# A second score buffer for the first units, the first loads in parts, and routing pieces turned by transposing DMAs

## The chip, the cores and the metric

One NeuronCore of a Trainium2 chip runs the whole program. The core has a matrix engine (TensorE, PE in the profile, with its weight loads as PEld), a vector engine (VectorE, DVE), an activation engine (ScalarE, ACT), a general engine (GpSimd, POOL) and a synchronisation engine (SyncE, SP) that mostly issues DMAs. SBUF is the on-chip memory, PSUM the banks into which PE accumulates. The metric is the device time of one execution in microseconds (us); lower is better.

## What is computed

Three stages follow each other; the second and third take the rows that the one before made.

```python
# 1: attention over 4 batches x 8 heads, 576 rows of 64; scores within tau of the row's maximum are kept
scores = scale * q @ k.T
thresh = max(scores, -1) - tau
scores = where(scores >= thresh, scores, -1e9)
attn = exp(scores - max(scores)) / (sum + 1e-9)
x = (attn @ v)                     # laid out as 2304 x 512
# 2: the mixture
h = x @ w_in                       # 512 -> 2048
x = (h - tanh(h)) @ w_out          # 2048 -> 512
# 3: the experts, one per row
logits = x @ w_gate;  e_idx = argmax(logits, 1)     # 8 experts
gate_w = softmax(logits)[e_idx];  eom = sigmoid(x @ w_output_gate)
for e in range(8):                 # rows with e_idx == e only
    out[mask] = gate_w * eom[:, e] * (relu(x[mask] @ w1[e]) @ w2[e])     # 512 -> 1024 -> 512
```

## The kernel before

The order of all work is made when the program is built, by a list planner written in Python (class `Sched`). Each operation is added with `sc.add(engine, planned duration, due time, function, reads, writes)`; a DMA with `dma(...)`, which adds the issue on its queue. Buffers are rings: `buf(pool, tag, n, shape)` gives the next of n buffers, and its first writer waits for the users of the one n places back. The planner walks through all operations greedily, in several rounds, and writes an order for each engine; each engine then runs its own in order. So a change of one operation, of a buffer count or of a due time moves rows on every engine.

**Attention.** There are 32 units, each of one batch, one half of the rows and one pair of heads, with 4 or 5 tiles of 128 rows. For one tile PE makes the scores into a PSUM buffer `sp` of two banks (L939 in the first 8 units, L928 later), DVE takes the row's minimum of the negated scores and copies them to `em` (L948), ACT makes the exponential `e` (L951), ACT or POOL the threshold `tb` (L955, L959), DVE masks and multiplies (L961), PE transposes the result in four blocks (L998, L1015), ACT copies it out as `eth` (L422), and PE multiplies with v (L1030). There is one `sp` buffer: the scores of a tile wait until DVE has read those of the tile before. `raw_k`, `raw_v` and `raw_q` load k, v and q; the first q goes over the queue of ACT (L864), and tau over that of POOL (L393).

**Mixture.** The rows are cut in 9 chunks of 256. A step (`step`) takes a slice of the hidden size: PE makes `ph` (L604), ACT and DVE the function, PE adds it to two PSUM tiles `x2_0` and `x2_1` (L638). Some steps of chunks 0 to 6 run between attention units, with their PSUM pools `ps_x` (2 banks) and `ps_h` (1 bank) open from the start, beside the pools `ps_s`, `ps_t` and `ps_v` of the attention. Partial sums go to DRAM (`x2p`). After the attention the chunks are finished in the order of

```python
ORDER = ((7, 6), (0,), (1,), (2,), (3,), (4,), (5,), (8,))
```

**Routing.** `route` runs for each finished chunk, over its two tiles of 128 rows. DVE adds up or copies the tile into `xr` in SBUF (L690, L693), and SP stores it to DRAM as `x2f` (L694). PE turns `xr` in four blocks of 128x128 back into the same PSUM tile (L698), ACT takes the first bf16 piece `xs0` from there (L709), DVE the remainder `xd` (L711), DVE or ACT the second piece, DVE or POOL the third (L716). PE multiplies each piece with the gate weights in four matmuls (L723, tile `rt`), and from the logits come ranks (L769) and at last the lists of rows of each expert (L831). The last chunk routed, 8, is kept whole: it is turned too and goes straight on in f32.

**Experts.** `early_rows` reads the list that stands after chunk 5, gathers expert 0's rows from `x2f` by two indirect DMAs on POOL (L1162), and PE transposes them (L1169) for the first layer of expert 0 (L1193). The other experts follow to the end of the program.

Of the kernel before, what the change touches and what calls it, by code (L numbers as in the profile page):

```python
# [12 lines left out]
BF16 = mybir.dt.bfloat16  # L13
# [8 lines left out]
P = 128  # L22
# [27 lines left out]
HALVE = 400  # L50
FULL = 8
NHH = 12
NRAW = 2
# [268 lines left out]
def tile_main(ctx, tc, qa, qb, q2, kT, k3, vv, tau, w_in, w_out, gates, w1, w2, out, dbg=None):  # L322
# [69 lines left out]
    ext_m = sc.mem()  # L392
    nc.gpsimd.dma_start(tau_t, tau.to_broadcast([P, 1]))  # L393
    nc.scalar.activation(usum[:, 0:1], bsq, AF.Exp)
# [65 lines left out]
    a_ps = ExitStack()  # L460
    pools["ps_x"] = pool("ps_x", PS, stack=a_ps)
    pools["ps_h"] = pool("ps_h", PS, stack=a_ps)
    a_stack = ExitStack()
# [4 lines left out]
    for n_ in ("ps_s", "ps_t", "ps_v"):  # L468
        pools[n_] = pool(n_, PS, stack=at_stack)

# [204 lines left out]
    def route(c, due, x2, part, listed=True):  # L675
# [9 lines left out]
        for t in range(2):  # L685
            T = 2 * c + t
            xr = buf("rt", "xr", 3, [P, DM])
            if part:
                dma(due - 20000, lambda xr=xr, T=T: nc.sync.dma_start(xr.t, x2p[T]), [x2p_m[T]], [xr], 262144)
                sc.add("DVE", dve(512, True) + 5, due, lambda xr=xr, t=t: nc.vector.tensor_tensor(  # L690
                    out=xr.t, in0=x2[t].t, in1=xr.t, op=ALU.add), [x2[t]], [xr])
            else:
                sc.add("DVE", dve(512, True), due, lambda xr=xr, t=t: nc.vector.tensor_copy(xr.t, x2[t].t), [x2[t]], [xr])  # L693
            dma(due, lambda xr=xr, T=T: nc.sync.dma_start(x2f[T * P:(T + 1) * P, :], xr.t), [xr], [(x2f_m, T)], 262144)  # L694

            def turns(xr=xr, t=t):
                for k in range(4):
                    nc.tensor.transpose(x2[t].t[:, k * P:(k + 1) * P], xr.t[:, k * P:(k + 1) * P], ident)  # L698

            sc.add("PE", 434, due, turns, [xr], [x2[t]])  # L700
            xd = buf("rt", "xd", 2, [P, DM])
            if whole:
                xts.append(xd)
                sc.add("ACT", act(512, True), due, lambda xd=xd, t=t: nc.scalar.activation(
                    xd.t, x2[t].t, AF.Copy), [x2[t]], [xd])
                continue
            xs = [buf("rt", f"xs{k}", 2, [P, DM], BF16) for k in range(3)]
            xts.append(xs)
            sc.add("ACT", act(512, True), due, lambda xs=xs, t=t: nc.scalar.activation(  # L709
                xs[0].t, x2[t].t, AF.Copy), [x2[t]], [xs[0]])  # L710
            sc.add("DVE", dve(512, True) + 5, due, lambda xs=xs, xd=xd, t=t: nc.vector.tensor_tensor(  # L711
                out=xd.t, in0=x2[t].t, in1=xs[0].t, op=ALU.subtract), [x2[t], xs[0]], [xd])
            round_to("r_2", 512, due, lambda xs=xs: xs[1].t, lambda xd=xd: xd.t, [xd], [xs[1]])
            eng = pick("r_3")
            e_ = nc.vector if eng == "DVE" else nc.gpsimd
            sc.add(eng, dve(512) + 5 if eng == "DVE" else pool_tt(512), due, lambda xs=xs, xd=xd, e_=e_: e_.tensor_tensor(  # L716
                out=xs[2].t, in0=xd.t, in1=xs[1].t, op=ALU.subtract), [xd, xs[1]], [xs[2]], port=True)
        lg = buf("ps_r", "rt", 1, [P, 2, 48])
        g_, gr = gt_
        for t in range(2):  # L720
            def logits(k, t=t):
                for cc in range(4):
                    nc.tensor.matmul(  # L723
                        lg.t[:, t, 0:48 - 16 * k], xts[t][k].t[:, cc * P:(cc + 1) * P], g_.t[:, cc, 0:48 - 16 * k],
                        start=(k == 0 and cc == 0), stop=(k == 2 and cc == 3))
# [122 lines left out]
    def raw_k(b, hp, due):  # L848

        k_ = kst[b, hp] = buf("kv", "kst", 4, [P, 2, S])  # L850
        dma(due - 6000, lambda: nc.sync.dma_start(
            k_.t.rearrange("p a b -> p (a b)")[:, 0:3 * KB], k3[b, hp]), (), [k_], 3 * P * KB * 4)

# [4 lines left out]
    def raw_q(ui, due):  # L858
# [4 lines left out]
        eng = nc.sync if ui else nc.scalar  # L863
        dma(due - 6000, lambda: eng.dma_start(  # L864
            qh.t[:, 0:n], q2[b, hp, :, o:o + n]), (), [qh], 512 * n, "SP" if ui else "ACT")
        return qh, None
# [29 lines left out]
    def attention(ui, k0, qs):  # L896
# [12 lines left out]
        for qt in range(2 + half):  # L909
# [4 lines left out]
            for h in range(1 if merged else 2):  # L914
                d = T0 + k * TAU
                k += 1
                sp = buf("ps_s", "sp", 1, [P, 2, 512])
                mx = buf("sm", "mx", 8, [P, 1])
# [25 lines left out]
                if full:  # L944
                    sc.add("PE", 880, d - TAU // 2, scores_full, [qh, kb], [sp])
                else:
# [143 lines left out]
    for ui, (b, half, hp) in enumerate(units):  # L1090
# [20 lines left out]
        if ui < 4 and FULL < 8:  # L1111
            prep_k(b, hp, (starts[ui + 4] - 4) * TAU)
        sc.kind = "moe"
        for c in range(NCH):
            if ready[c] == ui:
# [668 lines left out]
```

## Time and profile before

| | us |
|---|---|
| runs, median (lowest to highest) | 986.95 (985.33 to 987.18) |
| the profiled execution | 984.61 |
| its span | 982.8 |
| PE busy | 950.9 |
| DVE busy | 708.2 |
| ACT busy | 560.0 |
| POOL busy | 400.1 |

The span is from the first to the last instruction in the profiler's record of one execution. Busy times of several engines overlap. The attention fills the time to some 480 us, with parts of the mixture between its units, the rest of the mixture and the routing run from there to some 735 us, and the experts to the end.

### The profile page before, as it was taken

To read this page: it belongs to the slowest core of one execution; us is meant where nothing else is said; L and a number is where in the kernel's file an instruction comes from. 1 tells how busy PE (TensorE), PEld (TensorE's weight loads), DVE (VectorE), ACT (ScalarE), POOL (GpSimd) and SP (SyncE) were. 2 spreads that over 40 slices of the span, in tenths; PEclk is the share of its full clock that TensorE was granted. 3 is DMA by queue.
4 is the path that set the end of the run, shared out by engine and by line. 5 is a ranking of instruction groups with operands and counts; after the bars stand their busy time and mean duration, and the time that the engine had idled before them with its cause. 6 is when DMAs were issued, how large, how long until landed. Compare 5 with 4: busy or idle time off the path is not lost.

```text
span 982.8 us, 18693 instructions
## 1 busy us (share of the span) xinstructions
PE 950.9 (97%) x6655; PEld 817.4 (83%) x6655; DVE 708.2 (72%) x1744; ACT 560.0 (57%) x1186; POOL 400.1 (41%) x603
## 2 busy tenths in 40 slices
PE   6889899999999999999999999999999999999997
PEld 3456678888888888888889888888898889999996
DVE  5889999989779775665278986698556786666630
ACT  5678878888787866766355434444333443444431
POOL 2457988889778865644300110011102320122101
PEclk9899999999999999999999999999999999999999
DMA  7365553654654762532582842231714766565501
GB/s 235 132 212 165 186 192 138 199 182 155 200 198 137 235 206 73 173 136 103 221 324 83 291 149 87 97 119 54 260 41 152 262 229 217 172 191 183 185 1 42
DMA packets 45015, 162.56 MB, mean 165 GB/s; under 512 B 6142, under 2 KB 6142, under 8 KB 39024
## 3 DMA queue, kind: packets, MB, share of 16 engines
q1 hardware_dynamic: 41472, 151.11, 46.0%
q0 software_dynamic: 3296, 9.90, 2.9%
q8 instruction: 54, 0.88, 0.4%
q10 hardware_dynamic: 144, 0.26, 0.1%
q14 instruction: 49, 0.40, 0.1%
HBM read 126.12 MB, written 35.59 MB: 165 GB/s over the span
## 4 chain that ended last, share of the span: by engine, by line
PE 81%; DVE 9%; issue 3%; ACT 2%; POOL 2%; DMA 1%; POOLq 0%; SPq 0%; DVEq 0%; ACTq 0%
PE ph L604 18%; PE x L638 18%; PE ph L1556 10%; PE py L1443 7%; PE pv L1030 7%; PE sp L928 6%; PE pt L998 5%; PE py L1589 3%; DVE em L961 3%; DVE em L948 2%; PE ph L1193 1%; DVE ct L552 1%; PE sp L939 1%; DVE ct L555 1%; PE pt L1488 1%
## 5 line engine op out<-in xcount | busy, mean ns | idle before, releaser
L604 PE MATMUL ph<-xh,wi 128*128 128x256 f32 x1152 | 181.8, 287 | 0.0
L638 PE MATMUL x<-wo,gh 128*128 128x512 f32 x576 | 169.0, 405 | 0.6 <-POOL gh L424 0.6
L961 DVE SCALAR_TENSOR_TENSOR em<-em,tb,e 128x576 f32<-128x576 f32 x144 | 140.5, 978 | 31.6 <-ACT e L951 18.0
L604 PEld LDWEIGHTS ph<-xh,wi 128*128 128x128 f32 x1152 | 156.8, 189 | 5.3 <-issue 0.9
L951 ACT ACTIVATE e<-em,mx 128x576 f32<-128x576 f32 x144 | 111.0, 772 | 46.3 <-DVE em L948 40.9
L948 DVE TENSOR_SCALAR_CACHE_REDUCE em<-sp 128x576 f32<-128x576 f32 x144 | 108.3, 752 | 36.8 <-PE sp L928 23.5
L424 POOL TENSOR_SCALAR gh<-u 128x512 fp32r<-128x512 f32 x52 | 40.2, 773 | 191.2 <-DVE u L627 128.0
L638 PEld LDWEIGHTS x<-wo,gh 128*128 128x128 f32 x576 | 98.9, 189 | 17.6 <-issue 1.8
L422 ACT ACTIVATE eth<-pt 128x512 f32<-128x512 f32 (+1 forms) x160 | 85.5, 549 | 24.8 <-PE pt L998 24.6
L998 PE MATMUL pt<-ident,em 128*128 128x128 f32 x576 | 88.6, 279 | 6.4 <-DVE em L961 4.2
L604 PE MATMUL ph<-xl,wi 128*128 128x256 f32 x576 | 94.5, 286 | 0.0
L638 PE MATMUL x<-wo,gl 128*128 128x512 f32 x288 | 92.8, 405 | 0.0
L617 ACT ACTIVATE u<-ph 128x512 f32<-128x512 f32 x72 | 42.8, 594 | 87.4 <-PE ph L604 81.2
L998 PEld LDWEIGHTS pt<-ident,em 128*128 128x128 f32 x576 | 68.8, 143 | 20.2 <-DVE em L961 10.1
L625 DVE SCALAR_TENSOR_TENSOR w<-w,u 128x512 f32<-128x512 f32 x72 | 51.4, 713 | 41.4 <-ACT w L621 41.1
L604 PEld LDWEIGHTS ph<-xl,wi 128*128 128x128 f32 x576 | 78.8, 189 | 1.1 <-issue 0.8
L442 DVE TENSOR_TENSOR w<-wraw,w 128x512 fp32r<-128x512 f32 x98 | 66.1, 692 | 11.8 <-ACT w L422 10.0
L928 PE MATMUL sp<-kst,qh 128*128 128x288 f32 (+2 forms) x252 | 72.9, 308 | 1.6 <-DVE em L948 1.4
L1030 PE MATMUL pv<-eth,vt 128*64 128x256 f32 (+1 forms) x512 | 70.9, 417 | 1.0 <-ACT elh L422 1.0
L1477 POOL DMA_INDIRECT rows<-x2f,gid x20 | 21.9, 1096 | 116.4 <-PE pt L1488 109.6
L928 PE MATMUL sp<-kst,ql 128*128 128x288 f32 (+2 forms) x252 | 67.9, 293 | 0.0
L638 PEld LDWEIGHTS x<-wo,gl 128*128 128x128 f32 x288 | 51.0, 189 | 9.7 <-issue 0.9
(372 smaller groups left out, 2051.2 us busy)
## 6 DMA issues: line engine op xcount, KB each, us to landing
wraw<-in_w_dram SPq DMA_DIRECT2D x64, 512.0 KB, 4.3
wi<-wsv SPq DMA_DIRECT2D x17, 1024.0 KB, 6.0
wo<-wsv SPq DMA_DIRECT2D x17, 1024.0 KB, 5.4
craw<-in_w_in_dram SPq DMA_DIRECT2D x14, 512.0 KB, 4.1
craw<-in_w_out_dram SPq DMA_DIRECT2D x14, 512.0 KB, 3.8
kr<-in_kT_dram SPq DMA_DIRECT2D x24, 288.0 KB, 4.4
wsv<-wi SPq DMA_DIRECT2D x6, 1024.0 KB, 4.3
wsv<-wo SPq DMA_DIRECT2D x6, 1024.0 KB, 5.6
```

Of the source, the lines that this page charges most:

```text
L422: return sc.add("ACT", act(n, psum), due, lambda: nc.scalar.activation(dst(), src(), AF.Copy), r, w)
L442: return sc.add(eng, dve(n, psum) + 5 if eng == "DVE" else pool_tt(n), due, lambda: e.tensor_tensor(out=dst(), in0=src(), in1=hi().bitcast ...
L604: nc.tensor.matmul(ph.t[:, j, :], wi.t[:, w_, cc * CH + j * P:cc * CH + (j + 1) * P], x_.t[:, cc, :], start=(n == 0 and cc == 0), stop=(n ...
L638: nc.tensor.matmul(x2b[c, half][t].t, g_.t[:, j, t * P:(t + 1) * P], wo.t[:, w_, j * DM:(j + 1) * DM], start=(first and n == 0 and j == 0) ...
L928: nc.tensor.matmul(sp.t[:, kb_, o:o + w], q_.t[:, q0:q0 + P], kb.t[:, hh, c0:c0 + w], start=(i == 0), stop=(i == len(todo) - 1),)
L948: sc.add("DVE", 665, d, lambda ev=ev, sp=sp, mx=mx: nc.vector.tensor_scalar(out=ev().rearrange("p (a b) -> p a b", a=2), in0=sp.t[:, :, 0: ...
L951: sc.add("ACT", 667, d + 800, lambda e=e, ev=ev, mx=mx: nc.scalar.activation(e.t, ev(), AF.Exp, bias=mx.t, scale=-1.0), [(em, h), mx], [e])
L961: sc.add("DVE", 729, d + TAU, lambda ev=ev, tb=tb, e=e, rs=rs, h=h: nc.vector.scalar_tensor_tensor(out=ev(), in0=ev(), scalar=tb.t, in1=e. ...
L998: nc.tensor.matmul(pt.t[:, kt, :], em.t[:, c0:c0 + P], ident, is_transpose=True, start=(kt == 0), stop=(kt == 3))
L1030: nc.tensor.matmul(pvf()[h * D:(h + 1) * D], vb_.t[:, k, :], eth[h].t[:, kt, 0:n] if kt < 4 else elh.t[:, 0:n], start=(kt == 0), stop=(kt ...
L1443: nc.tensor.matmul(py[k].t[:, 0:cap], wx()[:, k * P:(k + 1) * P], x_.t[:, 0:cap], start=(f == 0 and n == 0), stop=(f == 7 and n == 2))
L1556: nc.tensor.matmul(ph.t[:, 0:cap], wx()[:, cc * P:(cc + 1) * P], x_.t[:, cc, 0:cap], start=(n == 0 and cc == 0), stop=(n == 2 and cc == 3))
```

## The change

It has two parts that the diff keeps apart.

The first is at the start of the program. A pool `ps_e` with a second `sp` buffer takes the banks of `ps_x` and `ps_h` for units 0 to 3 (`EARLY`), in which every other tile uses it; a barrier (`to_a`) closes it after unit 3 and opens the mixture's pools, and the steps are held behind that barrier (`sc.gate`). The first load of k is cut into three parts, the third due later, the first load of q into two, and the scores depend on the parts that they read. The load of tau goes from POOL's queue to ACT's.

The second is in `route`. For the eight chunks routed before the last, PE does not turn `xr`. The pieces are made from `xr` in SBUF, and each bf16 piece of 128x512 is turned by a DMA that transposes while it copies (`dma_start_transpose`, on SP) into `xt`, from which the logits read. The last chunk keeps its turns on PE. The ring of `xr` goes from 3 buffers to 2, those of the pieces from 2 to 1, and `xt` has 2 of each.

```diff
+EARLY = 4
-    nc.gpsimd.dma_start(tau_t, tau.to_broadcast([P, 1]))
+    nc.scalar.dma_start(tau_t, tau.to_broadcast([P, 1]))
...
-    pools["ps_x"] = pool("ps_x", PS, stack=a_ps)
-    pools["ps_h"] = pool("ps_h", PS, stack=a_ps)
+    e_ps = ExitStack()
+    pools["ps_e"] = pool("ps_e", PS, stack=e_ps)
...
+    def to_a():
+        e_ps.close()
+        pools["ps_x"] = pool("ps_x", PS, stack=a_ps)
+        pools["ps_h"] = pool("ps_h", PS, stack=a_ps)
...
-            xr = buf("rt", "xr", 3, [P, DM])
+            xr = buf("rt", "xr", 2, [P, DM])
...
-            sc.add("PE", 434, due, turns, [xr], [x2[t]])
             xd = buf("rt", "xd", 2, [P, DM])
             if whole:
+                def turns(xr=xr, t=t):
...
+                sc.add("PE", 434, due, turns, [xr], [x2[t]])
                 xts.append(xd)
...
-            xs = [buf("rt", f"xs{k}", 2, [P, DM], BF16) for k in range(3)]
-            xts.append(xs)
-            sc.add("ACT", act(512, True), due, lambda xs=xs, t=t: nc.scalar.activation(
-                xs[0].t, x2[t].t, AF.Copy), [x2[t]], [xs[0]])
-            sc.add("DVE", dve(512, True) + 5, due, lambda xs=xs, xd=xd, t=t: nc.vector.tensor_tensor(
-                out=xd.t, in0=x2[t].t, in1=xs[0].t, op=ALU.subtract), [x2[t], xs[0]], [xd])
+            xs = [buf("rt", f"xs{k}", 1, [P, DM], BF16) for k in range(3)]
+            xt_ = [buf("rt", f"xt{k}", 2, [P, 4, P], BF16) for k in range(3)]
+            xts.append(xt_)
+            sc.add("ACT", act(512), due, lambda xs=xs, xr=xr: nc.scalar.activation(
+                xs[0].t, xr.t, AF.Copy), [xr], [xs[0]])
+            sc.add("DVE", dve(512) + 5, due, lambda xs=xs, xd=xd, xr=xr: nc.vector.tensor_tensor(
+                out=xd.t, in0=xr.t, in1=xs[0].t, op=ALU.subtract), [xr, xs[0]], [xd], port=True)
...
+            for k in range(3):
+                dma(due, lambda k=k, xs=xs, xt_=xt_: nc.sync.dma_start_transpose(xt_[k].t, xs[k].t), [xs[k]], [xt_[k]],
+                    262144, slack=600)
...
-                        lg.t[:, t, 0:48 - 16 * k], xts[t][k].t[:, cc * P:(cc + 1) * P], g_.t[:, cc, 0:48 - 16 * k],
+                        lg.t[:, t, 0:48 - 16 * k], xts[t][k].t[:, cc, :], g_.t[:, cc, 0:48 - 16 * k],
...
+        first = not (b or hp)
+        for j0, n, d in ((0, 1, 0), (1, 1, 0), (2, 1, TAU)) if first else ((0, 3, 0),):
...
+        for h in range(2 if not ui else 1):
+            cols = slice(h * 256, h * 256 + 256) if not ui else slice(0, n)
...
-                sp = buf("ps_s", "sp", 1, [P, 2, 512])
+                sp = buf("ps_e" if ui < EARLY and k % 2 == 0 else "ps_s", "sp", 1, [P, 2, 512])
...
+        if ui == EARLY - 1:
+            open_a = sc.barrier(to_a, 0, list(sc.ops))
...
+                    sc.gate = open_a
                     e_ = step(c, v[0], i == 0, i == n - 1, "ps_h", "ps_x", moe_due, span, "ga", 0)
+                    sc.gate = None
```

The planner's new orders are shown at four places. First PE at the start of the program, before and then now; a tile's scores are one row, `pt` and `pv` are transposes, the numbers tell buffers apart:

```order
L939 MATMUL sp_246<-kst_224,qh_222 128x288 x2
L939 MATMUL sp_260<-kst_224,qh_222 128x288 x2
L998 MATMUL pt_265<-ident_60,em_253 128x128 x4
L939 MATMUL sp_276<-kst_224,qh_222 128x288 x2
L998 MATMUL pt_286<-ident_60,em_253 128x128 x4
L1015 MATMUL pv_295<-ident_60,em_253 128x128
L939 MATMUL sp_300<-kst_224,qh_222 128x288 x2
```

```order
L956 MATMUL sp_234<-kst_221,qh_219 128x288 x2
L956 MATMUL sp_245<-kst_221,qh_219 128x288 x2
L956 MATMUL sp_260<-kst_221,qh_219 128x288 x2
L956 MATMUL sp_273<-kst_221,qh_219 128x288 x2
L1016 MATMUL pt_280<-ident_60,em_248 128x128 x4
L956 MATMUL sp_290<-kst_225,qh_227 128x288 x2
L1016 MATMUL pt_300<-ident_60,em_248 128x128 x4
```

Four tiles' scores stand ahead of the first transposes now, where two stood. Next ACT at its start, before and now:

```order
L864 DMA qh<-in_q_dram 128x512
L394 ACT_TABLE_LOAD
L394 ACTIVATE usum<-bsq 128x1
L951 ACTIVATE e<-em,mx 128x576 x2
L544 ACTIVATE ct<-craw 128x512
```

```order
L394 DMA tau_t<-in_tau_dram 128x1
L395 ACT_TABLE_LOAD
L395 ACTIVATE usum<-bsq 128x1
L880 DMA qh<-in_q_dram 128x256 x2
L969 ACTIVATE e<-em,mx 128x576 x3
```

The q loads stand behind the table load and an activation, where the one q load stood first. Next PE at the first routed chunk, before and now (`x_0` and `x_1` are the two x2 tiles, `rt` the logits):

```order
L638 MATMUL x_1_7042<-wo_7272,gl 128x512 x2
L698 MATMUL x_0_7024<-ident,xr 128x128 x4
L638 MATMUL x_1_6797<-wo_7272,gl 128x512 x2
L604 MATMUL ph<-xh,wi_6618 128x256 x4
L604 MATMUL ph<-xl,wi_6618 128x256 x4
L604 MATMUL ph<-xh,wi_6618 128x256 x4
L698 MATMUL x_1_7042<-ident,xr 128x128 x4
L723 LDWEIGHTS xs_7422
L723 MATMUL rt<-g_6965,xs_7422 128x48
```

```order
L644 MATMUL x_0_7532<-wo_6672,gh 128x512 x4
L644 MATMUL x_0_7532<-wo_6672,gl 128x512 x2
L644 MATMUL x_1_7544<-wo_6672,gh 128x512 x4
L644 MATMUL x_1_7544<-wo_6672,gl 128x512 x2
L610 MATMUL ph<-xh,wi_7166 128x256 x4
L733 LDWEIGHTS xt_7435
L733 MATMUL rt<-g_7037,xt_7435 128x48
```

The turns are gone, and the logits of a tile stand behind later steps' matmuls: between a tile's last x2 matmul and its first logits there are from 40 matmuls of 256 columns with 22 of 512 up to three times as many. Last SP where the routing begins, before and now (`x2f` is the store of a tile, `wraw`, `wi` and `wo` are weights):

```order
L525 DMA wo_9485<-wsv_1_205 128x2048
L525 DMA wi_9522<-wsv_0_208 128x2048
L525 DMA wo_9547<-wsv_1_207 128x2048
L525 DMA wo_9597<-wsv_1_209 128x2048
L694 DMA x2f<-xr 128x512 x2
```

```order
L726 DMA_TRANSPOSE xt_7435<-xs_7423 128x4x128
L700 DMA x2f<-xr 128x512
L726 DMA_TRANSPOSE xt_7478<-xs_7469 128x4x128
L726 DMA_TRANSPOSE xt_7493<-xs_7476 128x4x128
L1301 DMA wraw<-in_w_dram 128x1024
L531 DMA wo_7509<-wsv_1_208 128x2048
```

Three transposing DMAs for each tile stand between stores and weight loads now, 48 in all, where SP had the stores alone.

## Rows read from the trace of the kernel before

**Rows 1.** The page, section 1: busy us, share of the span, instructions.

```profile
PE 950.9 (97%) x6655; PEld 817.4 (83%) x6655; DVE 708.2 (72%) x1744; ACT 560.0 (57%) x1186; POOL 400.1 (41%) x603
```

**Rows 2.** Windows: stretch, us, busy per engine, TensorE clock, DMA share, GB/s.

```profile
0.00:60.00 60.00, 44.53 (x254) 25.36 (x255) 44.55 (x127) 36.76 (x74) 22.10 (x51) 0.94 0.57 182
60.00:120.00 60.00, 55.58 (x380) 36.68 (x378) 55.91 (x128) 50.47 (x107) 47.78 (x72) 0.97 0.60 186
120.00:180.00 60.00, 57.93 (x422) 47.74 (x420) 57.28 (x125) 49.23 (x108) 51.64 (x77) 1.00 0.48 162
180.00:240.00 60.00, 59.51 (x432) 50.19 (x432) 53.84 (x119) 49.72 (x107) 51.22 (x77) 1.00 0.63 201
600.00:660.00 60.00, 59.99 (x467) 53.08 (x467) 44.39 (x164) 24.18 (x52) 6.89 (x8) 1.00 0.30 106
```

**Rows 3.** Timeline of PE, first and last of 16 turns: start us, us, instruction.

```profile
553.96 0.60 PE L698 MATMUL x<-ident,xr 128*128 128x128 f32 x4
554.31 0.71 PE L638 MATMUL x<-wo,gl 128*128 128x512 f32 x2
...
686.20 0.60 PE L698 MATMUL x<-ident,xr 128*128 128x128 f32 x4
686.63 0.26 PE L723 MATMUL rt<-g,xs 128*128 128x48 bf16 x4
```

**Rows 4.** Groups by line and form, 480 to 730 us: busy us, mean ns, idle before.

```profile
L711 DVE TENSOR_TENSOR xd<-x,xs 128x512 f32<-128x512 f32 x16 | 10.9, 684 | 1.1 <-ACT xs L709 1.1
L716 POOL TENSOR_TENSOR xs<-xd,xs 128x512 bf16<-128x512 f32 x8 | 9.8, 1224 | 36.1 <-DVE xs L426 29.5 <-PE rt L775 6.6
L709 ACT ACTIVATE xs<-x 128x512 bf16<-128x512 f32 x16 | 9.5, 596 | 19.7 <-PE x L698 18.2 <-DVE xs L426 1.5
```

**Rows 5.** DMA issues: count, KB each, median us from issue to landing.

```profile
x2f<-xr SPq DMA_DIRECT2D x18, 256.0 KB, 2.0
x2p<-xo SPq DMA_DIRECT2D x14, 256.0 KB, 6.2
xr<-x2p SPq DMA_DIRECT2D x14, 256.0 KB, 2.7
...
qh<-in_q_dram SPq DMA_DIRECT2D x3, 256.0 KB, 4.6
...
rows<-x2f,gid POOLq DMA_INDIRECT x20, 4.0
```

**Rows 6.** Chain of waits, 510 to 530 us: start us, us, what.

```profile
519.69 2.87 PE ph L604 x24
522.56 2.79 PE x L638 x12
```

**Rows 7.** Timeline around the list and the gathers of expert 0.

```profile
696.40 0.22 PE L831 MATMUL lst<-pb,pa 128*128 128x48 bf16 x2
...
701.09 1.01 POOL L1162 DMA_INDIRECT xd<-x2f,ge  x1 [0.30 <-issue]
...
723.50 1.04 PE L1169 MATMUL x<-ident,xd 128*128 128x128 f32 x8
```

**Rows 8.** Waits of DVE, 0 to 60 us: total us, times, longest us.

```profile
DVE em L948 <- PE sp L939: 6.5, 4, 5.0
DVE em L961 <- ACT e L951: 3.3, 4, 1.0
...
DVE em L961 <- ACT tb L955: 1.0, 1, 1.0
...
DVE em L961 <- POOL tb L959: 0.7, 1, 0.7
```

**Rows 9.** Timeline of the first microseconds.

```profile
0.73 0.39 ACTq L864 DMA_DIRECT2D qh<-in_q_dram  x1
...
1.16 1.28 ACT L394 ACT_TABLE_LOAD   x1 [1.16 <-PEq L1773]
...
5.32 0.53 PEld L939 LDWEIGHTS sp<-kst,qh 64*128 64x128 f32 x4 [5.32 <-DMA qh<-in_q_dram]
```

More of the change, by code (lines that the diff above doesn't have):

```diff
@@ L468, in tile_main @@
     for n_ in ("ps_s", "ps_t", "ps_v"):
-        pools[n_] = pool(n_, PS, stack=at_stack)
+        pools[n_] = pool(n_, PS, side="right", stack=at_stack)
+    def to_a():
+        e_ps.close()
+        pools["ps_x"] = pool("ps_x", PS, stack=a_ps)
+        pools["ps_h"] = pool("ps_h", PS, stack=a_ps)
     xc = {}
@@ L694, in route @@
             dma(due, lambda xr=xr, T=T: nc.sync.dma_start(x2f[T * P:(T + 1) * P, :], xr.t), [xr], [(x2f_m, T)], 262144)
-            def turns(xr=xr, t=t):
-                for k in range(4):
-                    nc.tensor.transpose(x2[t].t[:, k * P:(k + 1) * P], xr.t[:, k * P:(k + 1) * P], ident)
-            sc.add("PE", 434, due, turns, [xr], [x2[t]])
             xd = buf("rt", "xd", 2, [P, DM])
             if whole:
+                def turns(xr=xr, t=t):
+                    for k in range(4):
+                        nc.tensor.transpose(x2[t].t[:, k * P:(k + 1) * P], xr.t[:, k * P:(k + 1) * P], ident)
+                sc.add("PE", 434, due, turns, [xr], [x2[t]])
                 xts.append(xd)
@@ L850, in raw_k @@
         k_ = kst[b, hp] = buf("kv", "kst", 4, [P, 2, S])
-        dma(due - 6000, lambda: nc.sync.dma_start(
-            k_.t.rearrange("p a b -> p (a b)")[:, 0:3 * KB], k3[b, hp]), (), [k_], 3 * P * KB * 4)
+        first = not (b or hp)
+        for j0, n, d in ((0, 1, 0), (1, 1, 0), (2, 1, TAU)) if first else ((0, 3, 0),):
+            cols = slice(j0 * KB, (j0 + n) * KB)
+            dma(due - 6000 + d, lambda cols=cols: nc.sync.dma_start(
+                k_.t.rearrange("p a b -> p (a b)")[:, cols], k3[b, hp, :, cols]), (),
+                [(k_, j) for j in range(j0, j0 + n)], n * P * KB * 4)
     def raw_v(b, hp, due):
@@ L863, in raw_q @@
         eng = nc.sync if ui else nc.scalar
-        dma(due - 6000, lambda: eng.dma_start(
-            qh.t[:, 0:n], q2[b, hp, :, o:o + n]), (), [qh], 512 * n, "SP" if ui else "ACT")
+        for h in range(2 if not ui else 1):
+            cols = slice(h * 256, h * 256 + 256) if not ui else slice(0, n)
+            dma(due - 6000, lambda cols=cols: eng.dma_start(
+                qh.t[:, cols], q2[b, hp, :, o + cols.start:o + cols.stop]), (),
+                [(qh, j) for j in ((h,) if not ui else (0, 1))], 512 * (cols.stop - cols.start), "SP" if ui else "ACT")
         return qh, None
@@ L944, in attention @@
                 if full:
-                    sc.add("PE", 880, d - TAU // 2, scores_full, [qh, kb], [sp])
+                    sc.add("PE", 880, d - TAU // 2, scores_full,
+                           [(qh, 0), (qh, 1), (kb, 0), (kb, 2)] if merged else [(qh, h), (kb, h)], [sp])
                 else:
```

## The prediction

> **What bounds the kernel now.** I read the page's busy times first, then the busy time by stretch, then who waits for whom in the stretches that the change touches. TensorE (PE) is busy for 950.9 of 982.8 us [rows 1], so some 32 us of the span are left in which it does nothing. The stretches say where [rows 2]: the first 60 us hold 44.53 us of PE work, so 15.5 us of the 32 are there; 60 to 120 lacks 4.4 and 120 to 180 another 2.1 us, and VectorE (DVE) stands at 55.91 and 57.28 of 60 in these. From 180 us on PE is nearly full (59.51), and 600 to 660 us, in the middle of the routing, shows 59.99 of 60. Two rules follow. In the routing the time falls by what is taken off PE, one for one, and an operation on another engine costs nothing until PE waits for it. At the start the time falls only if the idle time of PE shrinks, and behind the first microseconds that goes by DVE, which holds the attention back there.
>
> The profiled execution took 984.61 us for a span of 982.8 us; the median of the runs is 986.95 us. I make the sum against 984.61 and add 2.34 us at the end.
>
> **Part 1, the routing.** Of nine chunks of 256 rows eight lose their turns on PE: 2 tiles each, so 16 groups of four 128x128 transposes. The rows show the first and the last of these [rows 3]. From the start of a group to the start of the next work on PE it is 0.35 us at 553.96, 0.43 at 686.20. Over all 16 the sum is 6.4 us (the modelled ends overlap, so the distance of the starts is the price, not the 0.60 us of the row). None of it hides behind anything, because PE is full there [rows 2]. The term is **-6.4 us**.
>
> What is added: the pieces are made out of SBUF in place of PSUM, by the same operations in the same number (ACT 596 ns, DVE 684 ns, POOL 1224 ns, [rows 4]); ACT has 24 of 60 us to do there and DVE 44 [rows 2], so I cost a different source at nothing. Each tile then issues three transposing DMAs on SP, 48 in all, and the logits matmul takes their result. In the trace no such DMA appears. The nearest rows are moves of 256 KB, twice the size of a bf16 piece: the x2f store lands 2.0 us after its issue, loads of that size 2.7 to 4.6 us, a gather of 128 scattered rows 4.0, the slowest store 6.2 [rows 5]. I take 2.7 (a load into SBUF in the same stretch; ends 2.0 and 6.2). It costs time only if PE reaches the logits first. From a tile's last x2 matmul to its third piece it is xr, xs0, xd, xs1, xs2: 0.7 + 0.6 + 0.7 + 0.6 + 1.2 = 3.8 us (xr as xd, xs1 as xs0), and I put the handing over at 0.6 us more; with 2.7 us of DMA that is 7.1 us. The new order leaves between a tile's last x2 matmul and its first logits at the tightest place 40 matmuls of 256 columns and 22 of 512. The pace of PE is 2.87 us for 24 and 2.79 us for 12 [rows 6], so that is 4.8 + 5.1 = 9.9 us; elsewhere it is 10 to 31 us. So even 5.5 us of landing would be covered, and I cost the wait at nothing. The end of 6.2 us costs 0.7 us at the tight place, and 0 elsewhere.
>
> One advance is to be looked at apart: the list of expert 0's rows comes from the last of the routed chunks that count for it, and the gathers wait for it. Before, the list's matmul starts at 696.40, the second gather issues at 701.09, PE takes the gathered rows at 723.50 [rows 7]. With 4.0 us to land [rows 5] the chain is 8.7 us long, and 27 us stood there. In the new order 48 matmuls of 256 columns and 22 of 512 stand there, 5.7 + 5.1 = 10.9 us. So 2.2 us of slack are left of some 18; no cost, but this cover is thin.
>
> SP is moved past too: 48 issues stand between stores and weight loads. A transposing DMA waits on SP for its piece, and behind it stand the next weight loads (the order shows a wraw and a wo behind the first tile's three). The wait ends when the piece is there, some microseconds at most, and the loads are issued well ahead of use; cost nothing, end +2 us.
>
> Here a rule of the notes speaks against the change. The rows give 0.35 and 0.43 us for a group of four transposes on PE [rows 3]. The Trainium skill, VectorE: DVE Perf Modes, section on the three transpose paths, puts a 128x128 bf16 transpose at 390 ns on TensorE and at 1309 ns through the DMA crossbar, so the change trades a cheap path for a dear one. An estimate by that page is 4 x 1309 ns = 5.2 us for a piece: covered by the 5.5 us above if the three pieces of a tile fly together, but 48 x 5.2 = 251 us if they go one at a time (rival D would then end near 1085 us). No run here shows it yet.
>
> **Part 2, the start.** The order shows PE with the scores of four tiles ahead of the first transposes, where it had two, and DVE with the next tile's row minimum (L948) in the place of a wait. In the first 60 us DVE waits 6.5 us for scores, 5.0 of them ahead of the very first tile, which a second buffer cannot help; 1.5 us remain. For the exponential on ACT it waits 3.3 us and for the threshold 1.7 [rows 8]. A DVE that has another tile's scores lying ready can fill all of these: 1.5 + 3.3 + 1.7 = 6.5 us. But the buffer serves units 0 to 3 only, the weight conversions that used to fill such holes move to later rows, and the mixture's first steps may not start until unit 3 is done, since its banks lend the buffer. I take half of it and a little: **-3.5 us**, ends 0 and -6.5. It reaches the end because DVE is the fuller engine until past 120 us, with PE short of work [rows 2], so all behind it comes earlier.
>
> **Part 3, the first loads.** Before, ACT issues the q load at 0.73 us, ahead of its table load at 1.16 (1.28 us), and PE's first weight load waits for q until 5.32 us: 4.6 us from issue [rows 9]. Now the tau load stands first, then the table load and one activation, then two half loads of q. So the q issue slips to about 2.65 us, the second half to 3.0. With 2.7 us to land it is there at 5.7, with 2.0 at 5.0, with the 4.6 of the crowded start at 7.6. The first k parts are a third as large and are early enough. I take 5.7, **+0.4 us**, ends -0.3 and +2.3. What the earlier issue of tau saves is inside part 2's 1.7 us for thresholds and not counted twice.
>
> **The sum.** -6.4 - 3.5 + 0.4 = -9.5 us, so 984.61 - 9.5 = 975.1 in the profiled execution's terms and 977.5 us as a median.
>
> **Rivals.** (A) The forecast, -5 to -14 us: 973 to 982 us.
>
> (B) The start does not do what it says: the planner's new order, the gate on the mixture's steps and the later q load eat the gain. Then the routing's -6.4 us is left, give or take 2: 979 to 983 us. For it speaks that the gate keeps PE from filling holes in the stretch with most of them; against it that DVE, not PE, is behind there.
>
> (C) No difference: a little of everything, late logits at some tiles, a start that loses 2 to 5 us since q comes at 7.6 us and steps start later. 985 to 989 us.
>
> (D) Slower: the transposing DMAs run one after another. From the first turn at 553.96 [rows 3] to expert 0's list at 696.40 [rows 7] there are 142.4 us for 48 of them, 3.0 us each. With the slack of 2.2 us at the list and the 9.5 us gained it ends above the time before from 154/48 = 3.2 us each. At 4.0 us, the gather's time [rows 5], it is 192 - 142 = 50 us of lateness, less 12: some 1025 us. At 2.7 us nothing is seen. Against it: the DMA engines were busy for 0.30 of 600 to 660 us [rows 2], so transfers have room to run side by side. For it: nothing here shows the transposing kind.
>
> (E) Slower by a little: expert 0's rows come late. Above 2.2 us of slip each microsecond costs one on PE, so a list that slips by 15 us (transposing DMAs of 6.2 us that also wait in SP's queue behind others) gives 984.6 - 9.5 + 12.8 + 2.3 = 990 us.
>
> **How the numbers follow.** Chances: A 0.50, B 0.22, C 0.09, D 0.11, E 0.08. Likeliest is A, and its middle is **977.5 us**. The range holds A with its ends (the start at -6.5 us and the q load at -0.3: 984.61 - 13.2 + 2.3 = 973.7; another 4 us where the new order packs the time behind 60 us better than I count, since 60 to 120 alone lacks 4.4 us of PE work, so 969), B, C and E up to 990; D is left out: **969 to 990 us**. A difference of 0.2%, 2 us, is about what a measurement of this kernel can tell from none. Faster by more: A and B, 0.72, and a part of C, so 0.73. Within: 0.09. Slower by more: D, E and a rest of C, 0.18.
>
> **What would show it.** In the profile after: no transposes on PE under the routing but for the last chunk's 8, and PE at 59.9 of 60 or more between 540 and 735 us (if it waits there for a DMA into xt, D or E holds, and the time from issue to landing of these DMAs decides). The first PE work at 5.0 to 7.6 us. DVE in 0 to 60 us at 48 us or more in place of 44.55, with less waiting for ACT e. The list of expert 0 to its first transposes without a PE wait. Wrong would be: DVE as idle as before at the start (then B), or PE in the first 150 us with less work than before.

## The result and the profile after

| | before | after |
|---|---|---|
| runs, median (lowest to highest), us | 986.61 (985.33 to 987.18) | 975.29 (974.41 to 978.73) |
| ratio, 95% interval | | 0.9894 (0.9867 to 0.9920) |
| the profiled execution, us | 984.61 | 974.67 |
| its span, us | 982.8 | 972.9 |
| PE busy, us | 950.9 | 943.0 |
| experts' first matmul at, us | 730.04 | 720.12 |

The change makes the kernel faster by 10.4 us, by the ratio (the medians differ by 11.3); 977.5 was predicted, 975.29 came. The median before is over four runs here; the 986.95 that the prediction went by was over three of them. The two spans differ by 9.9 us, and all of that is there when the experts begin; behind it both kernels take 252.8 us.

First the stretches of the kernel after, to be held beside [rows 2]; the columns are the same.

```profile
0.00:60.00 60.00, 50.82 (x333) 29.48 (x333) 49.51 (x144) 44.00 (x92) 29.01 (x57) 1.00 0.58 189
60.00:120.00 60.00, 50.36 (x324) 33.38 (x325) 51.09 (x123) 44.98 (x96) 43.66 (x72) 0.94 0.57 185
600.00:660.00 60.00, 60.00 (x483) 51.89 (x481) 48.58 (x183) 25.59 (x58) 9.40 (x10) 1.00 0.72 177
```

The first 60 us hold 6.3 us more of PE work and 5.0 us more of DVE work than before. The next 60 hold 5.2 us less of PE work: most of the head start is not kept. A row at a low clock counts more busy time for the same work; with what the clock loses taken off (3.4 us before and none after up to 60 us, 5.1 and 3.4 up to 120, counted below), PE is some 9.7 us ahead at 60 us and 2.8 at 120. In the routing PE is as full as it was, and the DMA engines are at 0.72 of the time instead of 0.30.

Then the waits of DVE in the first 60 us (answering [rows 8]), and the start of the timeline (answering [rows 9]):

```profile
DVE em L966 <- PE sp L956: 8.9, 3, 4.9
DVE eps_t L350 <- PEq L1795: 0.8, 1, 0.8
DVE em L979 <- ACT e L969: 0.2, 1, 0.2
```

```profile
0.74 0.40 ACTq L394 DMA_DIRECT2D tau_t<-in_tau_dram  x1
1.17 1.28 ACT L395 ACT_TABLE_LOAD   x1 [1.17 <-PEq L1795]
1.24 0.90 ACTq L880 DMA_DIRECT2D qh<-in_q_dram  x2
...
5.33 1.33 PE L956 MATMUL sp<-kst,qh 64*128 64x288 f32 x4 [5.33 <-DMA qh<-in_q_dram]
```

The wait for the exponential went from 3.3 to 0.2 us, that for thresholds from 1.7 to nothing. That for scores rose, from 6.5 to 8.9 us, of which 4.9 are ahead of the first tile. The q loads issue at 1.24 us, while the table load still runs, and the first scores start when they did before.

Last the new transfers, from the list of DMA issues, and the way from the list of expert 0's rows to their transposes (answering [rows 7]):

```profile
x2f<-xr SPq DMA_DIRECT2D x18, 256.0 KB, 2.7
...
xr<-x2p SPq DMA_DIRECT2D x14, 256.0 KB, 3.1
...
xt<-xs SPq DMA_TRANSPOSE x48, 3.0
```

```profile
703.98 0.22 PE L841 MATMUL lst<-pb,pa 128*128 128x48 bf16 x2
...
707.15 1.03 POOL L1184 DMA_INDIRECT xd<-x2f,ge  x1 [0.31 <-issue]
...
715.00 0.60 PE L1191 MATMUL x<-ident,xd 128*128 128x128 f32 x4
```

A transposing DMA lands 3.0 us after its issue. PE reaches expert 0's rows 11.0 us after the list, and no wait of PE for `xt` or for the gathered rows stands in the profile.

### The profile page after: what moved, and what is told of

Same layout as the page of the kernel before. It is cut to its first block, busy times and chain, and to the rows that moved or that the text cites. A ratio compares the mean times of both kernels' runs of the same rounds, so it can differ in the third digit from the quotient of the medians.

```text
span 972.9 us, 18677 instructions
## 1 busy us (share of the span) xinstructions
PE 943.0 (97%) x6591; PEld 810.2 (83%) x6591; DVE 698.5 (72%) x1744; ACT 559.1 (57%) x1186; POOL 401.1 (41%) x602
## 4 chain that ended last, share of the span: by engine, by line
PE 84%; DVE 5%; ACT 3%; issue 3%; POOL 3%; DMA 1%; POOLq 0%; ACTq 0%; DVEq 0%
PE x L644 20%; PE ph L610 19%; PE ph L1578 10%; PE pv L1048 7%; PE py L1465 7%; PE sp L945 6%; PE pt L1016 5%; PE py L1611 3%; PE ph L1215 1%; DVE em L966 1%; DVE em L979 1%; PE sp L956 1%; PE pt L1510 1%; ACT eth L423 1%; PE pt L1479 1%
## 5 line engine op out<-in xcount | busy, mean ns | idle before, releaser
L644 PE MATMUL x<-wo,gh 128*128 128x512 f32 x576 | 171.9, 408 | 0.6 <-POOL gh L425 0.6
L979 DVE SCALAR_TENSOR_TENSOR em<-em,tb,e 128x576 f32<-128x576 f32 x144 | 133.9, 934 | 29.1 <-ACT e L969 16.2
L977 POOL TENSOR_TENSOR tb<-mx,tau_t 128x1 f32<-128x1 f32 x96 | 39.2, 408 | 53.0 <-DVE em L966 46.6
```

The costliest lines, as they stand in the source:

```text
L644: nc.tensor.matmul(x2b[c, half][t].t, g_.t[:, j, t * P:(t + 1) * P], wo.t[:, w_, j * DM:(j + 1) * DM], start=(first and n == 0 and j == 0) ...
L979: sc.add("DVE", 729, d + TAU, lambda ev=ev, tb=tb, e=e, rs=rs, h=h: nc.vector.scalar_tensor_tensor(out=ev(), in0=ev(), scalar=tb.t, in1=e. ...
```

## How the spans are counted

To compare kernels whose orders differ everywhere I split each profiled span into three parts, all from the busy times and from stretches of 2 us over the whole span. Idle is the span less PE's busy time. The clock loss is the sum, over the stretches in which PE works and whose granted clock is under 0.97, of 2 us times what the clock lacks to 1. The rest is PE's work at full clock; where PE also waits in a half-clock stretch, it comes out somewhat too small. Where the clock falls in these profiles, it falls to 0.50 (1.2 in place of 2.4 GHz), and the half-clock stretches last about 3.4, 6.8 or 10.2 us, a loss of 1.7, 3.4 or 5.1 us.

| kernel | span | idle | clock loss | work at full clock | median of runs | ratio, 95% interval |
|---|---|---|---|---|---|---|
| before | 982.8 | 31.9 | 5.1 | 945.8 | | |
| after | 972.9 | 29.9 | 3.4 | 939.6 | 975.29 | 0.9894 (0.9867 to 0.9920) |
| e1, routing alone | 979.1 | 32.2 | 5.0 | 941.9 | 980.89 | 0.9944 (0.9929 to 0.9959) |
| e2, start alone | 983.6 | 32.5 | 5.1 | 946.0 | 983.48 | 0.9962 (0.9947 to 0.9977) |
| e3, buffer alone | 974.1 | 28.7 | 0.0 | 945.4 | 976.07 | 0.9897 (0.9882 to 0.9912) |
| e4, loads alone | 984.5 | 32.6 | 6.8 | 945.1 | 986.74 | 1.0011 (0.9995 to 1.0027) |
| e9, buffer and routing | 970.2 | 29.7 | 1.7 | 938.8 | 971.17 | 0.9828 (0.9807 to 0.9850) |
| e10, after with filler | 974.3 | 25.5 | 3.4 | 945.4 | 976.07 | 0.9880 (0.9859 to 0.9900) |
| e6, turns twice | 992.5 | 33.8 | 6.8 | 951.9 | 995.98 | 1.0087 (1.0065 to 1.0109) |
| e5, third piece twice | 993.1 | 42.8 | 8.5 | 941.8 | 995.62 | 1.0085 (1.0059 to 1.0111) |
| e12, e9 with tau moved | 970.1 | 29.7 | 0.0 | 940.4 | 972.82 | 0.9851 (0.9831 to 0.9871) |
| e15, e9 with loads parted | 972.3 | 28.7 | 5.1 | 938.5 | 972.62 | 0.9842 (0.9821 to 0.9863) |
| e14, e9 with units 0 to 2 | 979.2 | 32.3 | 10.2 | 936.7 | 977.32 | 0.9888 (0.9871 to 0.9906) |
| e14, e9 with units 0 and 1 | 977.5 | 28.6 | 11.9 | 937.0 | 978.62 | 0.9901 (0.9885 to 0.9916) |

Ratios are to the kernel before, run beside it. The split is of one execution each.

Two more readings cover what one split cannot. The first divides each profiled span at the start of the attention's last matmul:

```profile
476.81 0.33 PE L1043 MATMUL pv<-sel,rb 128*128 128x64 f32 x2
473.36 0.33 PE L1061 MATMUL pv<-sel,rb 128*128 128x64 f32 x2
468.20 0.33 PE L1049 MATMUL pv<-sel,rb 128*128 128x64 f32 x2
470.19 0.33 PE L1053 MATMUL pv<-sel,rb 128*128 128x64 f32 x2
```

These are the kernels before and after, e3 and e9. The second takes the mean granted clock of every run, not only of the profiled one, and gives what it lacks to 1 as a share of the span. This loss also holds the end of the span, where the clock is low and PE has nothing left to do (1.2 to 2.4 us in the profiles above).

| kernel | attention's last matmul at | from there to the end | clock loss, mean of all runs |
|---|---|---|---|
| before | 476.81 | 506.0 | 5.8 (39 runs) |
| after | 473.36 | 499.5 | 6.6 |
| e1, routing alone | 478.73 | 500.4 | 5.4 |
| e2, start alone | 477.62 | 506.0 | 7.7 |
| e3, buffer alone | 468.20 | 505.9 | 2.1 |
| e4, loads alone | 478.93 | 505.6 | 8.5 |
| e9, buffer and routing | 470.19 | 500.0 | 2.9 |
| e10, after with filler | 474.55 | 499.8 | 5.4 |
| e6, turns twice | 479.51 | 513.0 | 6.8 |
| e5, third piece twice | 475.79 | 517.3 | 12.2 |
| e12, e9 with tau moved | 470.12 | 500.0 | 1.9 |
| e15, e9 with loads parted | 472.13 | 500.2 | 5.1 |
| e14, e9 with units 0 to 2 | 479.03 | 500.2 | 7.0 |
| e14, e9 with units 0 and 1 | 477.14 | 500.4 | 9.8 |

Behind the attention the four kernels with turns on PE take 505.6 to 506.0 us, and the eight in which the DMAs turn the pieces once take 499.5 to 500.4, whatever their start. So the routing's part is worth 5.2 to 6.5 us there, and all else that separates these twelve lies ahead of the attention's end. There one execution says less: e6 has the order of the kernel before on every engine up to the routing, and e5 that of the kernel after, and yet their attention ends 2.7 and 2.4 us later.

## The two halves apart

The first two runs each take one half of the diff of the change; the next two each take a half of the start.

**e1_routes:** the kernel before with the edits in `route` alone.

```diff
+            for k in range(3):
+                dma(due, lambda k=k, xs=xs, xt_=xt_: nc.sync.dma_start_transpose(xt_[k].t, xs[k].t), [xs[k]], [xt_[k]],
+                    262144, slack=600)
```

> The kernel before with the change of the routing alone (pieces out of SBUF, 48 transposing DMAs, the shorter rings). Theory A (the turns were pure PE time in a full stretch, and the transposing DMAs are covered): the time falls by the 6.4 us of the 16 groups, 0.9935 of before, the experts' first matmul comes 6.4 us earlier while the attention ends where it did (472.8 us). Rival B (the routing's order was re-planned for a better start, or the start's earlier end feeds the routing): less than 4 us here, the rest only together with the start. Rival C (transposing DMAs late): PE waits for xt in this stretch and the time does not fall.

0.9944, 5.5 us faster: theory A, whose 0.9935 lies in the interval; B and C fall. Behind the attention's end the profile is 5.6 us shorter than before, which fits. Only the attention's last v matmuls, at 474.43 us, come 1.9 us later than before (472.51), where theory A had them unmoved; that is within what one order showed above.

**e2_start:** the kernel before with all other edits of the change: `EARLY`, `ps_e`, the gate, the loads in parts, tau on ACT's queue.

> The kernel before with the other half of the change alone: the second score buffer for units 0 to 3, the loads in parts and tau on ACT's queue. Theory A (the two halves add): 3 to 4 us faster than before, 0.996 to 0.997, PE busy in 0 to 60 us near 50.8 instead of 44.5, the attention ends near 469 us. Rival B (the start gains nothing by itself, all is the routing): 0.2% at most, attention's end at 472 us or later. Together with the routing alone the two ratios should multiply to 0.9894 if they add.

0.9962, 3.7 us faster. The product of the two ratios is 0.9906 against 0.9894 for the whole: the halves add within the intervals. But the profiled execution, the slowest of the six, has a longer span than before (983.6), with two half-clock stretches and no less idle time, and its attention ends 0.8 us later, not some 4 us earlier as theory A had it; PE's 50.77 us of work in the first 60 came as expected. So this gain is not a tidy one.

**e3_buffer** takes `EARLY`, `ps_e` and the gate of the diff, and **e4_loads** takes the loads and tau.

> The kernel before with the second score buffer alone, first loads whole and tau on POOL's queue as before. Theory A (the buffer fills the waits of DVE for scores, exponential and threshold): most of the gain of the start, 2 to 4 us. Rival B (the loads are what does it, since the second tile's k and q are there earlier): under 1 us.

> The kernel before with the loads alone: k in three parts, q in two, tau on ACT's queue; one score buffer. Theory A (the first scores still start at 5.3 us, so the loads give nothing): within 1 us of before, and what is beyond that is the new order of the whole program. Rival B (the earlier tau and the smaller parts give the gain): 2 us or more faster.

The buffer alone gives 10.2 us, far beyond what theory A allowed, as much as the whole change. The loads alone give nothing that can be measured. Of the 8.7 us by which e3's profiled span is shorter, 3.2 are idle time of PE and 5.1 the clock loss: no half-clock stretch is left. Over all runs the spans differ by 10.5 us in the mean and the clock loss by 3.8 (5.9 in the 17 runs of the kernel before beside it, 2.1 in e3). So the clock, which the prediction never looked at, goes with a third or more of this gain. That it causes so much is not shown: in e1 runs of the same span (979.1 us) had a mean clock of 0.992 and of 0.997.

The stretches in which the clock fell before, and those in which it falls after, one profile each:

```profile
24.00:28.00 4.00, 1.70 (x10) 0.67 (x10) 3.44 (x9) 2.52 (x5) 1.36 (x3) 1.00 0.24 68
28.00:32.00 4.00, 3.66 (x15) 2.17 (x17) 3.30 (x10) 2.55 (x6) 2.66 (x4) 0.52 0.45 146
32.00:36.00 4.00, 4.00 (x24) 1.99 (x22) 2.94 (x11) 2.79 (x6) 0.61 (x3) 0.63 0.61 251
```

```profile
92.00:96.00 4.00, 2.66 (x20) 1.85 (x19) 3.63 (x9) 2.81 (x6) 3.75 (x8) 1.00 0.65 157
96.00:100.00 4.00, 2.51 (x20) 1.49 (x18) 3.83 (x9) 3.64 (x7) 2.82 (x5) 0.94 0.19 41
100.00:104.00 4.00, 3.03 (x11) 2.51 (x11) 3.45 (x11) 2.71 (x6) 2.99 (x8) 0.50 0.80 326
104.00:108.00 4.00, 4.00 (x21) 2.93 (x21) 2.53 (x7) 2.89 (x7) 2.79 (x3) 0.70 0.30 94
```

Before, PE is busy for 1.70 of 4 us and then runs at half clock while it catches up; after, that place is filled, but the same happens at 100 us behind two slack stretches. Not every slack stretch is followed by a fall. In the kernel after, the clock stays at 1.00 in this one and in the stretch behind it:

```profile
84.00:88.00 4.00, 2.11 (x13) 1.09 (x11) 3.97 (x10) 3.88 (x10) 3.12 (x5) 1.00 0.25 74
```

## What the start's other edits take back

**e9_buffer_routes** is the kernel before with the buffer and the routing, the first loads as they were. Against the kernel after, in short:

```diff
-    nc.scalar.dma_start(tau_t, tau.to_broadcast([P, 1]))
+    nc.gpsimd.dma_start(tau_t, tau.to_broadcast([P, 1]))
...
-        first = not (b or hp)
-        for j0, n, d in ((0, 1, 0), (1, 1, 0), (2, 1, TAU)) if first else ((0, 3, 0),):
...
+        dma(due - 6000, lambda: nc.sync.dma_start(
+            k_.t.rearrange("p a b -> p (a b)")[:, 0:3 * KB], k3[b, hp]), (), [k_], 3 * P * KB * 4)
...
-        for h in range(2 if not ui else 1):
...
+        dma(due - 6000, lambda: eng.dma_start(
+            qh.t[:, 0:n], q2[b, hp, :, o:o + n]), (), [qh], 512 * n, "SP" if ui else "ACT")
```

> The changed kernel without its loads: the second score buffer and the routing's transposing DMAs, but k and q loaded whole and tau on POOL's queue as before. Theory A (the loads are not neutral in this order: they bring TensorE's half-clock stretch at 100 us that the buffer alone does not show, and some idle time): 0.9897 times 0.9944, so about 971 us, faster than the changed kernel by 4 us. Rival B (the buffer alone was a lucky order, which the routing's new plan undoes): 975 us or more, with a half-clock stretch again.

971.17 us, 0.9828; its interval ends below that of the change. Buffer and routing multiply (0.9897 x 0.9944 = 0.9842), so the loads of the change cost some 4 us in the median, 6.5 by the ratios. One half-clock stretch is there again, so B is right in that and wrong in the time. This version beats both kernels. Over all runs its clock loss is 2.9 us, and 6.6 in the kernel after: 3.7 of the 4.8 us between their mean spans. Between 60 and 100 us PE does 35.76 us of work in it, and 31.45 in the kernel after, which had done 2.1 us more up to 60 us; the first row is of e9, the second of after:

```profile
60.00:100.00 40.00, 35.76 (x243) 23.08 (x239) 37.48 (x87) 33.58 (x73) 36.33 (x53) 1.00 0.60 186
```

```profile
60.00:100.00 40.00, 31.45 (x212) 19.26 (x212) 35.70 (x80) 30.63 (x65) 31.38 (x50) 0.99 0.52 166
```

e9 and e3 have nearly the same PE work up to 100 us (84.5 and 84.0 us); from 108 us on they part. First e3, then e9:

```profile
108.00:112.00 4.00, 2.64 (x17) 1.97 (x17) 3.81 (x11) 3.48 (x9) 3.87 (x7) 1.00 0.74 183
112.00:116.00 4.00, 4.00 (x33) 2.72 (x33) 3.92 (x12) 3.00 (x8) 2.40 (x4) 1.00 0.89 315
```

```profile
108.00:112.00 4.00, 1.63 (x10) 1.09 (x9) 3.77 (x7) 2.80 (x7) 3.32 (x8) 0.99 0.81 211
112.00:116.00 4.00, 3.86 (x20) 2.59 (x22) 3.92 (x12) 3.03 (x7) 0.82 (x2) 0.58 0.63 228
```

In e3, with 2.64 us of work in the four, the clock stays; in e9, with 1.63, it falls behind them, a loss of 1.7 us in this execution.

Is it the transfers themselves or the order that comes with them? **e12_with_tau** moves the load of tau in e9, and the order of PE, DVE and SP stays the same row for row. **e15_parts** parts the first loads of e9 inside one planned operation each:

```diff
+        cuts = [slice(j * KB, (j + 1) * KB) for j in range(3)] if not (b or hp) else [slice(0, 3 * KB)]
...
+        qcuts = [(0, n)] if ui else [(0, 256), (256, n)]
```

> The version with the buffer and the routing (e9), plus the load of tau moved to ACT's queue ahead of q, and nothing else: the order of PE, DVE and SP stays row for row what it is in e9, so only the DMA itself moves. Theory A (the loads as transfers are neutral, what costs 4 us is the order that the planner makes once the loads are parted): 971 us as e9, first matmul within 0.5 us of e9's. Rival B (the q load behind tau and the table load is late): first matmul some 1 to 2 us later, 972 to 973 us.

> The version with the buffer and the routing (e9), whose first k load is issued as three DMAs and the first q load as two, inside one planned operation, so that the order of all engines stays that of e9 but for the added issues. Theory A (parted loads are neutral or a little better as transfers; the order is what costs): 970 to 972 us. Rival B (parted loads cost time at the start themselves): 974 us or more, like the changed kernel.

First PE row of e9, of e12 and of e15:

```profile
5.18 3.52 PE L949 MATMUL sp<-kst,qh 64*128 64x288 f32 x12 [5.18 <-DMA kst<-in_k_dram]
```

```profile
7.57 2.29 PE L949 MATMUL sp<-kst,qh 64*128 64x288 f32 x8 [7.57 <-DMA qh<-in_q_dram]
```

```profile
3.88 3.52 PE L951 MATMUL sp<-kst,qh 64*128 64x288 f32 x12 [3.88 <-DMA kst<-in_k_dram]
...
9.00 0.19 POOL L971 TENSOR_TENSOR tb<-mx,tau_t 128x1 f32<-128x1 f32 x1 [6.00 <-DMA tau_t<-in_tau_dram]
```

With tau in front PE waits for the whole q load and starts 2.4 us later: rival B of e12 is right about the place, and its 972 to 973 us hold the median, 1.65 us above e9, though the intervals overlap. Parted loads are there 1.3 us earlier, but then the first threshold waits for tau until 9.0 us (8.55 in e9), and the median is 1.45 us above e9 and 0.6 above theory A's range, again with intervals that overlap. DVE's first masking tells what is left: it starts at 8.78 us in e9, 10.63 in e12, 9.23 in e15 and 9.17 in the kernel after. So the loads of the change, taken as transfers, put it back by 0.4 us. Neither run reaches the 4 us. What costs the more is thus the order that the planner makes with the parted loads, with its lower clock; that fits e12 and e15, which keep e9's order, but it is shown by exclusion only, since both loads together in e9's order were not run.

**e14** changes only the number of units with the buffer:

```diff
-EARLY = 4
+EARLY = 3
```

> The version with the buffer and the routing (e9), the second buffer for units 0 to 2 instead of 0 to 3. The first 40 us are nearly the same work in nearly the same order, and what comes later is planned anew. Theory A (how the time behind 60 us falls out, in idle time of PE and half-clock stretches, is the planner's luck, a few us either way): between 969 and 977 us, with a number of half-clock stretches other than one. Rival B (the gain goes by the number of units that have the buffer): about 0.9 us above e9, a quarter of the 3.5.

> As e14_early3, with the second buffer for units 0 and 1 only. Theory A (luck of the order behind 60 us): 969 to 977 us and no row with the number of units. Rival B (the gain goes by the number of units): about 1.8 us above e9, and e14_early3 between the two.

977.32 and 978.62 us, so 6.1 and 7.4 us above e9. Neither theory holds whole: the time rises with fewer units, as B says, but by several times its 0.9 and 1.8 us; both medians lie just above theory A's range; and between the two runs themselves the intervals overlap. What rises in the profiles is the clock loss, by 8.5 and 10.2 us, but both profiles are of the slowest run of their kernel. Over all runs it rises by 4.1 and 6.9 us, of 6.7 and 7.4 us in the mean span. Work at full clock is lower here than in e9. The loss differs between executions of one kernel, and the time follows it in some kernels only: e4's twelve runs go from 985.25 us at a mean clock of 0.993 to 992.71 at 0.988, while the kernel before was at 986.39 us with 0.991 and at 989.18 with 0.995.

**e10_fill** gives PE something to do in the holes between 60 and 100 us of the kernel after:

```diff
+                    for kt in range(2 if 2 <= ui < 8 else 0):
+                        nc.tensor.matmul(pt.t[:, kt, :], ident, ident, is_transpose=True, start=True, stop=True)
```

> The changed kernel, with two transposes of the identity ahead of each group of turns of the score tiles in units 2 to 7, into the PSUM tile that the group overwrites: work for PE that waits for no other engine and whose result nobody reads, some 0.55 us a tile, where PE waits for DVE anyway. Theory A (PE's idle time in 60 to 100 us is what the clock falls after): no stretch below a granted clock of 0.9 near 100 us, and the time falls by up to 1.7 us or stays, though PE has some 15 us more to do. Rival B (the clock has nothing to do with it): the half-clock stretch stays and the time rises by whatever of the added work does not fit into waits, 2 us or more.

976.07 us and 0.9880 beside 0.9894: the 5.8 us of added work (some 15 were expected) cost nothing that can be measured, since idle time fell by 4.4. But two half-clock stretches remain, behind holes that the filler did not reach (0.84 us of work in 88 to 90, 0.85 in 102 to 104). This run does not decide on the clock, since slack was left.

## The price of the turns and the cover of the transfers

**e6_turns_twice** doubles the term of the routing in the kernel before:

```diff
-                for k in range(4):
+                for k in list(range(4)) * (1 if whole else 2):
```

> The kernel before with each of the 16 groups of four turns made twice, the same matmuls into the same PSUM tile; all else in its order. This measures the term of the turns by itself: theory A (each group costs its distance of starts in a full stretch): 16 more groups cost 16 x 4 x 0.12 to 0.27 us, 6 to 9 us more than before, near 1.0065. Rival B (the turns lie in slack, since ACT and DVE wait beside them): within 2 us.

The ratio says 8.6 us slower, at the upper end of theory A (whose 6 to 9 us go with 0.10 to 0.14 us for a transpose; 0.27 would give 17). The profiled spans differ by 9.7 us: 6.1 are PE's work at full clock (945.8 to 951.9), the 6.4 of the sum within what the split can tell, 1.7 another half-clock stretch, at 18 us, and 1.9 idle time. Behind the attention's end it is 7.0 us; the other 2.7 lie ahead of it, where nothing was changed. Theory A holds, B falls.

**e5_third_twice** makes the third piece of each tile late:

```diff
-                dma(due, lambda k=k, xs=xs, xt_=xt_: nc.sync.dma_start_transpose(xt_[k].t, xs[k].t), [xs[k]], [xt_[k]],
+                dma(due, lambda k=k, xs=xs, xt_=xt_: [nc.sync.dma_start_transpose(xt_[k].t, xs[k].t) for _ in range(2 if k == 2 else 1)][-1], [xs[k]], [xt_[k]],
```

> The changed kernel with the transposing DMA of each tile's third piece issued twice into the same buffer, so that it lands later by a whole landing and an issue, some 4.2 us, 16 times. Theory A (the 9.9 us and more of PE work between a tile's last x2 matmul and its logits cover a landing of 5.5 us for the first and more for the third piece): within 2 us of the changed kernel, PE busy 59.9 of 60 us in the routing. Rival B (the cover is used up): PE waits for xt at each tile, up to 16 x 4.2 = 67 us.

995.62 us, by the ratios 19 us above the kernel after, between the theories. The waits of SP and of PE in 540 to 720 us:

```profile
SPq L726 <- DMA xt<-xs: 40.4, 16, 5.3
SPq L726 <- ACT xs L716: 8.4, 6, 3.7
```

```profile
PE rt L733 <- DMA xt<-xs: 8.5, 9, 1.8
PE x L644 <- DVE gh L427: 3.6, 2, 1.9
```

The second DMA into a buffer waits on SP for the first, 2.5 us each, and everything behind it on SP waits too. PE then stands still for 12.9 us more than in the kernel after (idle 42.8 and 29.9). The clock loss is 5.1 us higher, but only 1.7 of that is in the routing, at 622 us; the rest falls ahead of the first transposing DMA. Behind the attention's end the kernel is 17.8 us longer. So the cover that I had counted, PE's work between a tile's last x2 matmul and its logits, does not hold for a queue that is held: 16 holds of 2.5 us used it up. A third piece that is late without holding SP was not run. What rival D feared, transposing DMAs that wait for one another, does cost time; in the change no wait of SP for a DMA into `xt` stands in the profile.

## Why the prediction was right, and where its steps were not

- **The sum** was -9.5 us; the profiled spans differ by 9.9, the ratio says 10.4. Forecast A holds. The mechanism of the routing was right; that the start came out near its term is luck, as below.
- **Part 1**, -6.4 us (the sixteen distances of starts sum to 6.46): 5.5 us alone (e1), 7.0 us behind the attention's end when doubled (e6), 6.5 us less there in the change (506.0 to 499.5). The full stretch made each piece of PE work count one for one, as [rows 2] had it.
- **The cover of the transfers** was right in its result. They land after 3.0 us, I took 2.7; from the list to expert 0's rows it is 11.0 us of which 6.9 are needed (second gather issued 3.17 us after the list, 3.7 to land in the list of issues), so 4.1 us of slack where I said 2.2. What I left out was SP: a transposing issue holds it for 1.2 us where a plain one took 0.4. e5 shows how thin the cover is on that side.
- **The rule of the Trainium skill** against the change (VectorE: DVE Perf Modes, The three transpose paths) gives 1309 ns for one 128x128 block through the DMA crossbar; 5.2 us for a piece was an estimate from it. This trace does not agree with that estimate: a piece of four blocks lands in 3.0 us, counted from its issue. The measurement decides.
- **Part 2**, -3.5 us: the size is that of e2 (3.7), and the attention of the change ends 3.4 us earlier (476.81 to 473.36), but this is luck: it is a balance of two larger things that I did not see, 10.2 us from the buffer alone (e3) and 6.5 taken back when the loads are added to it (e2). That DVE's waits for exponential and thresholds go was right (3.3 to 0.2 and 1.7 to 0 us); that those for scores shrink too was not (6.5 to 8.9). The step that failed is that the gain carries through to the end because all behind it comes earlier: 6.3 us of PE's busy time were won up to 60 us and 5.2 given back up to 120. The clock was no term of the sum, though [rows 2] showed 0.94 and 0.97. By the one profile of each, its loss falls from 5.1 to 3.4 us, but over all runs the change loses no less by it than the kernel before (6.6 and 5.8 us), while the buffer without the loads loses 2.1 (e3) and 2.9 (e9).
- **Part 3**, +0.4 us: measured 0.0 (5.32 and 5.33). The mechanism was wrong. The q load does not wait for the table load but issues at 1.24 us; behind tau it makes PE 2.4 us late if it is whole (e12), and with k and q in parts that is made up for.
- **Rivals.** B (start without effect), C, D and E did not happen, though B's doubt, that the new order eats the gain of the start, came true in large part. D and E shared another, and e5 shows that it was well placed.

What stays open is how far the half-clock stretches belong to an order and how far to an execution, and how much of the time they cause. They follow slack stretches of PE in every profile here, and the mean over all runs differs between orders (0.998 in e3, 0.990 in e14 with two units), but runs of one kernel differ by up to 0.008 of mean clock, and no run held the order and the waits fixed and changed the clock alone.

## What to carry to other kernels

In a stretch where PE is full, moving its transposes to another unit is worth their distance of starts, provided that the transfers neither reach PE late nor hold their queue for one another. In a stretch where PE waits, read the granted clock beside the idle time, and over all runs: here the profiled execution alone gave the change a gain by the clock that the other runs do not have. Divide the span where the edited stage begins: behind the attention twelve kernels fell into two groups within 1 us. And when a planner writes the order, run each edit alone: here the loads undid over a third of what buffer and routing gave.

## What was not expected of the hardware

- A transposing DMA of 128 KB holds SP for 1.19 to 3.1 us at the issue (median 1.21) and lands in 2.3 to 9.0 us (median 3.0), as long as a plain load of 256 KB (3.1). With 48 of them the share of the DMA engines in 600 to 660 us rose from 0.30 to 0.72, and the packets under 512 bytes from 6142 to 32414.
- DMAs that ACT issues were not held up by its table load here: they issue at 1.24 us, with the table load from 1.17 to 2.45.
- Where PE had work, the granted clock fell to half (0.50) only in the first 150 us, in which it has slack, but for one stretch of 3.4 us in e5 behind waits at 622 us. The kernels here lost from 0.0 (e3, e12) to 11.9 us (e14 with two units) by it in their profiles.
